# Attention and a gated feed-forward block on one core: the late score rounds, the splits of attention rows and the last two down projections rearranged

## The chip, the cores and the metric

The kernel runs on one core of a Trainium2 chip. The metric is the device time of one execution in microseconds (us). Before the change it is 1312.54 us, the median of three runs (1311.17 to 1313.77). A profile shows one further execution; the engines are called TensorE (PE, with its weight loads as PEld), VectorE (DVE), ScalarE (ACT), GpSimd (POOL) and SyncE (SP, which here only starts DMAs).

## The reference

One input x (2048 rows of 448) goes through two branches, and a gate per row mixes them:

```
g = sigmoid((x * gate_w).sum(-1))
a = attention(x)            # 16 heads of 28, softmax(q k^T / sqrt(28)) v, then @ wo
b = (relu(x W_gate) * (x W_up)) W_down      # 1792 hidden columns
out = g * a + (1 - g) * b
```

All data are float32. The kernel multiplies in a float32 form that keeps fewer bits, so most operands are split into a "high" part (a copy in that form) and a "low" part (the rest), and a product is a sum of a few matmuls of highs and lows.

## The kernel before, in words

Everything is ordered by hand: the program's text gives, engine by engine, the order in which instructions stand, and an engine never passes one of its own that waits. The same holds for the DMA starts on SP and on POOL.

**Projections.** q, k and v are made first and q, k are written to DRAM, from where each head's K and Q are loaded.

**Rounds.** Then come rounds (`ROUNDS`, line 46). A round is a string of letters that TensorE follows:

- `s` is one score matmul (`scores`, line 168): 128 keys by 512 queries into one PSUM bank, then ScalarE's exponential (line 175) into P. Four `s` make a key tile.
- `m` is a pair of matmuls (`smax`, line 139) whose maximum VectorE takes over 128x1024. The maxima of a head are subtracted, by two more rows of K and Q, when its scores are made.
- `x` is one matmul of the feed-forward block (`gu_mm`, line 380). Eleven fill a bank with 128 hidden columns of gate or up for 512 rows; two such units make a hidden tile. After the gate unit comes `relu` (line 391, ScalarE), after the up unit `spill_h` (line 398): a multiply on VectorE and a DMA to DRAM on POOL.

At a round's end the weights of the next units are split (`split_f`, line 364: highs on ScalarE, lows on POOL), and `pv` (line 408) multiplies P and V of the round's key tiles into `po`. A round scores one tile ahead of the tiles whose `pv` ends it; nine slots hold P. `small_things` (line 463) stands every four tiles and starts loads, row sums and the scaling of heads that are done. The last six rounds (`LATE`, line 44) have no maxima left: four tiles and two units each. Their scores alternate between two single banks (`ps_s`) and their units use a half of the double banks (`ps_w`) that the maxima had. `split_wo` (line 454) splits the output projection's weights, highs on ScalarE and lows on POOL, behind the `pv` of tile 248.

**Feed-forward end.** When the rounds are over, their memory is given back and a list (`todo`, line 617) sets the order. It has `gate_up` for the hidden tiles that are left, `down` (line 599: 12 matmuls that add one hidden tile to four banks of 128 rows) for all 56 tiles, in four groups of 512 rows, and for each group `fetch_o` (line 539, SP), two calls of `split_o` (line 546: ScalarE high, POOL low of 128x1024) and four of `wout` (line 553: 11 matmuls with WO, then VectorE's multiplication by the gate). Ahead of `down(i)` stand `fetch_d(i + 4)` (line 581, SP: down weights `wdr`, hidden tile `hr`) and `split_d(i + 2)` (line 589: WD's cast on VectorE and low on POOL, `hh`'s high on ScalarE and low on VectorE). After the last `down` of a group VectorE adds both branches (line 612) and a DMA writes each block of 128 rows.

Of the kernel before, what the change touches and what calls it, by code (L numbers as in the profile page):

```python
# [8 lines left out]
F32 = mybir.dt.float32  # L9
F32R = mybir.dt.float32r  # L10
BF16 = mybir.dt.bfloat16
AF = mybir.ActivationFunctionType
OP = mybir.AluOpType
# [5 lines left out]
P = 128  # L19
S = 2048  # L20
D = 448
# [3 lines left out]
GD = G * DH  # L25
F = 1792
NF = F // P
NB = 4
TB = 512
NK = S // P  # L30
SCALE = DH ** -0.5
# [7 lines left out]
SHORT = "smsxxsmsxsmsxmsxsmsxxsmsxsmsxxsmsxs"  # L39

LONG = "ssmmxsxxsxsmxxsxsmsxxsxxsmmsxxsxxsxsmsxxsmsmsxsxxsxmsmsxxxxsmxssxxmsxsmsxxsmsxmss"
WIDE = "msxxsmsxsxmsxxsxmsxxxxmssmxsxxsxxsmxmssxxxxsxsmsmsxxxxsxsmsxmsxxsxxxsmsmxxxsxsxxxsxmssxmxxss"

LATE = "sxsxxsxsxxsxsxxsxsxxsxsxxsxsxxsxsxsxsx"

ROUNDS = [(SHORT, 0), (SHORT, 1)] + [(LONG, 3)] * 9 + ([(WIDE, 4)] + [(LONG, 3)] * 8) * 2 + [(WIDE, 4)] + [(LATE, 2)] * 6
NP = 9


# [6 lines left out]
PARTS = [(0, 0), (0, 1), (1, 0)]  # L56
# [3 lines left out]
def gated_mix_kernel(ctx, tc, x, wq, wo, wgu, wd, out):  # L60
    nc = tc.nc
# [10 lines left out]
    def ps_s(name):  # L72
        return psum.tile([P, TB], F32, tag="s", bufs=2, name=name)

    def ps_w(name):
        return psum.tile([P, 2, TB], F32, tag="mx", bufs=2, name=name)

    def ps_o(name):
        return psum.tile([P, TB], F32, tag="po", bufs=1, name=name)

    def ps_x(name):
        return psum.tile([P, TB], F32, tag="x", bufs=1, name=name)

    def act_high(dst, src):
        nc.scalar.activation(dst, src, AF.Copy)  # L85
# [4 lines left out]
    def low(dst, src, high):  # L90
        nc.vector.tensor_tensor(dst, src, f32(high), op=OP.subtract)  # L91
# [20 lines left out]
    K = [vp.tile([P, S], F32R, name=f"K{r}") for r in range(3)]  # L112

    def p_slot(k, name, dt=F32):
        if k in (5, 6):
            return V[:, k - 3].rearrange("p k h d -> p (k h d)").rearrange("p (j t) -> p j t", t=TB)
        return (vp if k < 5 else att).tile([P, 4, TB], dt, name=name, tag=f"P{k}", bufs=1)
# [7 lines left out]
    Q = {}  # L125
# [40 lines left out]
    PT = {}  # L166

    def scores(i, j):
        h, kt = divmod(i, NK)
        if j == 0:  # L170
            PT[i] = p_slot(i % NP, f"P_{i}")
        ps = ps_s(f"s_{i}_{j}")
        nc.tensor.matmul(ps, K[h % 3][:GD + 2, kt * P:(kt + 1) * P], Q[h][:GD + 2, j * TB:(j + 1) * TB],  # L173
                         start=True, stop=True)
        nc.scalar.activation(PT[i][:, j], ps, AF.Exp, scale=SCALE)  # L175

    X = {}

# [4 lines left out]
    with tc.tile_pool(name="qkv", bufs=1) as pa:  # L183
# [95 lines left out]
        ps = ps_o("warm_ps")  # L279
# [6 lines left out]
        gate = const.tile([P, 2, NK], F32, name="gate")  # L286
# [74 lines left out]
        WR[i] = fe.tile([P, 2, 4, P], F32, name=f"wgr_{i}", tag="wgr", bufs=2)  # L361
        nc.sync.dma_start(WR[i], wgu[i % NF])

    def split_f(i, low, part=(0, 1)):

        if part[0] == 0:
            WS[i] = fe.tile([P, 2, 7, P], F32R, name=f"wg_{i}", tag="wg", bufs=2)
        w, wr = WS[i], WR[i]
        for s in part:
            act_high(w[:, s, 0:3], wr[:, s, 0:3])  # L370
            low(w[:, s, 3:6], wr[:, s, 0:3], w[:, s, 0:3])
        if part[-1] == 1:
            act_high(w[:, :, 6], wr[:, :, 3])
            low(w[64:, :, 6], wr[64:, :, 3], w[64:, :, 6])
            del WR[i]

# [11 lines left out]

    RL = {}

    def relu(i, ps):
        RL[i] = fe.tile([P, TB], F32, name=f"rl_{i}", tag="rl", bufs=2)
        nc.scalar.activation(RL[i], ps, AF.Relu)

    def hidden(i, ps, h):
        nc.vector.tensor_tensor(h, ps, RL.pop(i), op=OP.mult)  # L396

    def spill_h(i, ps):
        h = fe.tile([P, TB], F32, name=f"h_{i}", tag="h", bufs=2)
        hidden(i, ps, h)  # L400
        h_d[i] = dram.tile([P, TB], F32, name=f"h_d_{i}")
        nc.gpsimd.dma_start(h_d[i], h)  # L402


    NI = H * NK
# [41 lines left out]
    def load_wo():  # L447
        r = f32(q_slot("wor"))
        nc.sync.dma_start(r[:, 0:3, :D], wo_d[0:3 * P].rearrange("(c p) n -> p c n", p=P))
        for a in (0, 64):  # L450
            nc.sync.dma_start(r[a:a + 64, 3, :D], wo_d[3 * P:])
        return r[:, :, :D]
# [6 lines left out]

    done = sum(n for _, n in ROUNDS) // 2  # L460
    nxt = parts = i0 = 0
# [26 lines left out]
    wor = None  # L488
    for r, (order, nu) in enumerate(ROUNDS):
        ni = order.count("s") // NB  # L490
        late = "m" not in order
        todo = list(range(nxt, nxt + nu))
        nxt += nu
        small_things(i0 // 4)
        if m % (2 * NK) == 0 and i0 <= NI - LEAD:
            smax_end(m // (2 * NK) - 1)
        if late and wor is None:
            wor = load_wo()
        ns = nx = 0
        for o in order:  # L500
            if o == "s":
                i, j = i0 + 1 + ns // NB, ns % NB
                if ns == 4 * NB:
                    small_things(i0 // 4 + 1)
                if i < NI:
                    scores(i, j)
                ns += 1
            elif o == "m":
                smax(m)
                m += 1  # L510
            elif nx < NT * nu:
                i, half = divmod(todo[nx // NT], 2)
                if nx % NT == 0:
                    ps = ps_w(f"gu_{i}_{half}")[:, 0] if late else ps_x(f"gu_{i}_{half}")
                gu_mm(ps, i, half, nx % NT)
                nx += 1
                if nx % NT == 0:
                    (spill_h if half else relu)(i, ps)

        ready = nxt + (ROUNDS[r + 1][1] if r + 1 < len(ROUNDS) else 2)  # L520
        ready += ready % 2
        while parts < ready:
            split_f(parts // 2, pool_low, (parts % 2,))
            parts += 1
            if parts % 2 == 0:
                fetch_f(parts // 2 + 1)
        for i in range(i0, i0 + ni):
            pv(i)
            if i == NI - NK // 2:
                split_wo(wor)  # L530
        i0 += ni
# [4 lines left out]
    pf = ctx.enter_context(tc.tile_pool(name="ffn", bufs=1))  # L536
    ON, OR, GA, DR, HH, ACC = {}, {}, {}, {}, {}, {}
# [7 lines left out]

    def split_o(tb, c):
        if c == 0:
            ON[tb] = tuple(pf.tile([P, 4, TB], F32R, name=f"on{k}_{tb}", tag=f"on{k}", bufs=1) for k in range(2))
        c = slice(c, c + 2)
        act_high(ON[tb][0][:, c], OR[tb][:, c])  # L550
        pool_low(ON[tb][1][:, c], OR[tb][:, c], ON[tb][0][:, c])
# [14 lines left out]

    def gate_up(i):
        if i + 1 < NB * NF:
            split_f(i + 1, low)
        if i + 3 < NB * NF:  # L570
            fetch_f(i + 3)
        ps = ps_w(f"gu_{i}")
        for s in range(2):
            for n in range(NT):
                gu_mm(ps[:, s], i, s, n)
        relu(i, ps[:, 0])
        spill_h(i, ps[:, 1])

    WD = pf.tile([P, NF, 2, D], F32R, name="WD")
# [9 lines left out]
    def split_d(i):  # L589
# [6 lines left out]
        act_high(HH[i][:, 0], h)  # L596
        low(HH[i][:, 1], h, HH[i][:, 0])

    def down(i):
        tb, f = divmod(i, NF)  # L600
        if f == 0:
            ACC[tb] = [ps_s(f"acc_{tb}_0"), ps_s(f"acc_{tb}_1"), ps_x(f"acc_{tb}_2"), ps_o(f"acc_{tb}_3")]
        hh = HH.pop(i)
        for t in range(4):
            for n, (a, b) in enumerate(PARTS):
                nc.tensor.matmul(ACC[tb][t][:, :D], hh[:, a, t * P:(t + 1) * P], WD[:, f, b],  # L606
                                 start=(f == 0 and n == 0), stop=(f == NF - 1 and n == 2))
        if f == NF - 1:
            for t in range(4):
                k = tb * 4 + t  # L610
                y = pf.tile([P, D], F32, name=f"y_{k}", tag="y", bufs=4)
                nc.vector.scalar_tensor_tensor(y, ACC[tb][t][:, :D], gate[:, 1, k:k + 1], GA[tb][:, t],
                                               op0=OP.mult, op1=OP.add)
                (nc.sync if tb == NB - 1 else nc.gpsimd).dma_start(out[k * P:(k + 1) * P, :], y)


    todo = [(gate_up, done), (row_sums, H - 1), (gate_up, done + 1)]
# [5 lines left out]
    def before(i, *new):  # L623
        n = todo.index((down, i))
        todo[n:n] = new
# [1 line left out]

    before(0, (spread, H - 1))
    before(1, (normalise, H - 1))
    for tb, load, split, at in ((0, 2, 3, (4, 5, 6, 7)), (1, 5, 8, (10, 11, 14, 14)), (2, 21, 24, (28,) * 4),  # L630
                                (3, 35, 38, (42,) * 4)):
        before(load, (fetch_o, tb))
        before(split, (split_o, tb, 0))
        before(split + 1, (split_o, tb, 2))
        for t, i in enumerate(at):
            before(i, (wout, tb, t))

# [48 lines left out]
```

## Time and profile before

| what | us |
|---|---|
| median of three runs | 1312.54 |
| the profiled execution | 1315.21 |
| its span | 1313.4 |
| six late rounds, first score part to last `po` | 1018.6 to 1097.6 |
| feed-forward end | 1097.6 to 1307.5 |
| last result's work on VectorE ends | 1308.25 |

Busy shares of the span: PE 99%, PEld 69%, DVE 61%, ACT 59%, POOL 27%. A matmul is counted as busy from its start to a modelled end, and the next one overlaps it, so a stretch in which TensorE runs at half its pace can still show as busy: the distance from one start to the next tells more. In the views, a row names the engine, the line of the code, the operation, the tile written and the tiles read; "[0.82 <-ACT on L85]" behind a row means that the engine stood idle for 0.82 us ahead of it, and that ScalarE's write of `on` (line 85 is the helper for all highs on ScalarE, 94 the one for lows on POOL, 88 for casts on VectorE) ended the wait.

### The profile page before, as it was taken

The numbers are of one execution on the slowest core, as the hardware profiler recorded it, in microseconds if no ns is written. First come the engines' busy times: TensorE is split into PE (matmuls) and PEld (weight loads), VectorE is DVE, ScalarE is ACT, GpSimd is POOL, SyncE is SP. The second block draws the span as 40 slices with busy tenths as digits, with TensorE's granted clock in tenths as the row PEclk, the third lists the DMA queues.
The fourth block names the chain that finished last, engine by engine and source line by source line (L and its number), as shares of the span: only waits on it lengthen the run. The fifth ranks groups of instructions, "written<-read, shape, count | busy, mean of one in ns | idle before, by whom it ended". The sixth has DMA issues, their size and how long they took to land.

```text
span 1313.4 us, 17652 instructions
## 1 busy us (share of the span) xinstructions
PE 1300.0 (99%) x6689; PEld 907.0 (69%) x6689; DVE 799.4 (61%) x811; ACT 770.5 (59%) x1454; POOL 360.8 (27%) x496
## 2 busy tenths in 40 slices
PE   9999999999999999999999999999999999999998
PEld 5888666666666666666666666666666556789997
DVE  6577776676767666766767676767666003663332
ACT  5212686667676676766767667676766785222121
POOL 3212113222222232332313222222322235451020
PEclk9999999999999999999999999999999999999999
DMA  8845515142343624142525324151431225534432
GB/s 294 287 166 219 168 58 106 58 110 67 87 86 91 171 63 89 57 97 66 136 68 158 81 72 97 48 105 41 113 108 55 100 64 180 190 114 147 141 103 74
DMA packets 53533, 148.87 MB, mean 113 GB/s; under 512 B 9992, under 2 KB 17096, under 8 KB 48840
## 3 DMA queue, kind: packets, MB, share of 16 engines
q1 hardware_dynamic: 36520, 98.80, 29.2%
q0 software_dynamic: 16928, 48.93, 10.4%
q8 instruction: 53, 0.87, 0.3%
q14 instruction: 32, 0.26, 0.1%
HBM read 102.06 MB, written 46.02 MB: 113 GB/s over the span
## 4 chain that ended last, share of the span: by engine, by line
PE 93%; DMA 3%; issue 1%; DVE 1%; POOL 1%; ACT 1%; SPq 0%; POOLq 0%; ACTq 0%; DVEq 0%
PE gu L383 21%; PE s L173 19%; PE sm L147 18%; PE po L413 17%; PE acc L606 10%; PE qk L253 3%; PE wo L558 3%; PE v L262 2%; DMA K<-qk_d 1%; DMA qk_d<-st 1%; POOL on L94 1%; DMA wr<-wq 0%; DMA xr<-x 0%; DMA wdr<-wd 0%; PE mt L157 0%
## 5 line engine op out<-in xcount | busy, mean ns | idle before, releaser
L149 DVE TENSOR_REDUCE mx<-sm 128x1 f32<-128x1024 f32 x512 | 610.9, 1220 | 189.5 <-PE sm L147 188.3
L175 ACT ACTIVATE P<-s 128x512 f32<-128x512 f32 x800 | 455.0, 597 | 111.1 <-PE s L173 76.1
L173 PE MATMUL s<-Q,K 114*128 114x512 f32 x1024 | 400.7, 405 | 0.4 <-ACT P L175 0.3
L383 PE MATMUL gu<-X,wg 128*128 128x512 f32 x1232 | 397.0, 396 | 0.0
L147 PE MATMUL sm<-K,Q 112*128 112x512 f32 x1024 | 312.2, 396 | 0.7 <-DMA K<-qk_d 0.5
L173 PEld LDWEIGHTS s<-Q,K 114*128 114x128 f32 x1024 | 190.6, 188 | 108.9 <-ACT P L175 53.1
L383 PEld LDWEIGHTS gu<-X,wg 128*128 128x128 f32 x1232 | 233.5, 190 | 43.9 <-issue 0.8
L147 PEld LDWEIGHTS sm<-K,Q 112*128 112x128 f32 x1024 | 193.0, 190 | 46.6 <-DVE mx L149 2.7
L413 PE MATMUL po<-P,V 128*32 128x512 f32 x1600 | 181.9, 594 | 0.0
L94 POOL TENSOR_TENSOR wg<-wgr,wg 128x384 fp32r<-128x384 f32 x153 | 142.2, 941 | 99.8 <-issue 48.7
L175 ACT ACTIVATE V<-s 128x512 f32<-128x512 f32 x224 | 128.2, 598 | 33.2 <-PE s L173 21.2
L402 POOL DMA_DIRECT2D h_d<-h x56 | 31.7, 566 | 412.2 <-DVE h L396 382.0
L606 PE MATMUL acc<-WD,hh 128*128 128x448 f32 x672 | 140.9, 368 | 0.0
L606 PEld LDWEIGHTS acc<-WD,hh 128*128 128x128 f32 x672 | 126.1, 188 | 12.8
L413 PEld LDWEIGHTS po<-P,V 128*32 128x32 f32 x1600 | 49.1, 110 | 110.5 <-issue 110.5
L85 ACT ACTIVATE hh<-hr 128x512 fp32r<-128x512 f32 x56 | 35.2, 631 | 122.4 <-PE acc L606 118.6
L91 DVE TENSOR_TENSOR hh<-hr,hh 128x512 fp32r<-128x512 f32 x56 | 53.7, 960 | 64.4 <-ACT hh L85 64.4
L396 DVE TENSOR_TENSOR h<-gu,rl 128x512 f32<-128x512 f32 x56 | 38.6, 689 | 87.5 <-PE gu L383 37.3
L253 PE MATMUL qk<-X,W 128*128 128x512 f32 x308 | 76.6, 397 | 2.0 <-ACT X L85 1.8
L253 PEld LDWEIGHTS qk<-X,W 128*128 128x128 f32 x308 | 57.3, 188 | 18.4 <-ACT X L85 2.9
L85 ACT ACTIVATE wg<-wgr 128x384 fp32r<-128x384 f32 x168 | 68.0, 489 | 0.0
L413 PE MATMUL po<-V 128*32 128x512 f32 x448 | 54.1, 594 | 0.0
(58 smaller groups left out, 573.6 us busy)
## 6 DMA issues: line engine op xcount, KB each, us to landing
wgr<-wgu SPq DMA_DIRECT2D x56, 512.0 KB
qk_d<-st POOLq DMA_DIRECT2D x28, 512.0 KB, 3.5
K<-qk_d SPq DMA_DIRECT2D x64, 224.0 KB
Q<-qk_d SPq DMA_DIRECT2D x64, 224.0 KB
h_d<-h POOLq DMA_DIRECT2D x56, 256.0 KB, 2.3
hr<-h_d SPq DMA_DIRECT2D x56, 256.0 KB
x_d<-X POOLq DMA_DIRECT2D x6, 1024.0 KB, 5.0
X<-x_d SPq DMA_DIRECT2D x24, 256.0 KB
```

The costliest lines, as they stand in the source:

```text
L85: nc.scalar.activation(dst, src, AF.Copy)
L91: nc.vector.tensor_tensor(dst, src, f32(high), op=OP.subtract)
L94: nc.gpsimd.tensor_tensor(dst, src, f32(high), op=OP.subtract)
L147: nc.tensor.matmul(ps[:, c, :], Q[h][:GD, u * P:(u + 1) * P], K[h % 3][:GD, k0:k0 + TB], start=True, stop=True)
L149: nc.vector.tensor_reduce(MX[h][:, 2 * u + half:2 * u + half + 1], ps, axis=AX.XY, op=OP.max)
L173: nc.tensor.matmul(ps, K[h % 3][:GD + 2, kt * P:(kt + 1) * P], Q[h][:GD + 2, j * TB:(j + 1) * TB], start=True, stop=True)
L175: nc.scalar.activation(PT[i][:, j], ps, AF.Exp, scale=SCALE)
L253: nc.tensor.matmul(ps, W[:, a, c * P:(c + 1) * P], xf(tb, b), start=(n == 0), stop=(n == NT - 1))
L383: nc.tensor.matmul(ps, WS[i][:, s, a], xf(i // NF, b), start=(n == 0), stop=(n == NT - 1))
L413: nc.tensor.matmul(PO[h][32 * j:32 * j + 32], V[:, h // 4 % 2, kt, h % 4], PT[i][:, j], start=(kt == 0), stop=(kt == NK - 1))
L558: nc.tensor.matmul(ps[:, t % 2, :D], ON[tb][b // 4][:, b % 4, t * P:(t + 1) * P], WO[:, a], start=(n == 0), stop=(n == NT - 1))
L606: nc.tensor.matmul(ACC[tb][t][:, :D], hh[:, a, t * P:(t + 1) * P], WD[:, f, b], start=(f == 0 and n == 0), stop=(f == NF - 1 and n == 2))
```

## The change

- Three late rounds of eight tiles and four units take the place of six of four and two. Scores are made in pairs: two matmuls into a double bank, then one exponential of 128x1024. The units use the single banks.
- In the late rounds `relu` and the highs of the weight splits move from ScalarE to VectorE. `split_wo` still stands behind tile 248's `pv`, which is now in the last round.
- The halves of `split_o` move in the list: for rows 0 ahead of the `gate_up` that precedes downs 3 and 4, for rows 1 ahead of downs 7 and 9 (8 and 9 before), rows 2 of 23 and 25 (24 and 25), rows 3 of 37 and 39 (38 and 39). `on` has two buffers for one.
- The last two downs of all, hidden tiles 54 and 55 of the list, run together by blocks of rows: the six matmuls of a block, then its result. The very last block's DMA is started by ScalarE.

```diff
-LATE = "sxsxxsxsxxsxsxxsxsxxsxsxxsxsxxsxsxsxsx"
-ROUNDS = ... + [(LATE, 2)] * 6
+LATE = "ssxxxssxxxssxxxssxx" * 4
+ROUNDS = ... + [(LATE, 4)] * 3
...
+    def scores_pair(i, j):
+        h, kt = divmod(i, NK)
+        if j == 0:
+            PT[i] = p_slot(i % NP, f"P_{i}")
+        ps = ps_w(f"s_{i}_{j}")
+        for c in range(2):
+            nc.tensor.matmul(ps[:, c], K[h % 3][:GD + 2, kt * P:(kt + 1) * P], Q[h][:GD + 2, (j + c) * TB:(j + c + 1) * TB],
+                             start=True, stop=True)
+        nc.scalar.activation(PT[i][:, j:j + 2], ps, AF.Exp, scale=SCALE)
...
-    def split_f(i, low, part=(0, 1)):
+    def split_f(i, high, low, part=(0, 1)):
...
-            act_high(w[:, s, 0:3], wr[:, s, 0:3])
+            high(w[:, s, 0:3], wr[:, s, 0:3])
...
-            act_high(w[:, :, 6], wr[:, :, 3])
+            high(w[:, :, 6], wr[:, :, 3])
...
-        nc.scalar.activation(RL[i], ps, AF.Relu)
+        if late:
+            nc.vector.tensor_scalar_max(RL[i], ps, 0.0)
+        else:
+            nc.scalar.activation(RL[i], ps, AF.Relu)
...
-                    ps = ps_w(f"gu_{i}_{half}")[:, 0] if late else ps_x(f"gu_{i}_{half}")
+                    ps = (ps_s if late else ps_x)(f"gu_{i}_{half}")
...
-            split_f(parts // 2, pool_low, (parts % 2,))
+            split_f(parts // 2, dve_high if late else act_high, pool_low, (parts % 2,))
...
-            ON[tb] = tuple(pf.tile([P, 4, TB], F32R, name=f"on{k}_{tb}", tag=f"on{k}", bufs=1) for k in range(2))
+            ON[tb] = tuple(pf.tile([P, 4, TB], F32R, name=f"on{k}_{tb}", tag=f"on{k}", bufs=2) for k in range(2))
...
+    LAST = range(NB * NF - 2, NB * NF)
...
-        for t in range(4):
-            for n, (a, b) in enumerate(PARTS):
-                nc.tensor.matmul(ACC[tb][t][:, :D], hh[:, a, t * P:(t + 1) * P], WD[:, f, b],
-                                 start=(f == 0 and n == 0), stop=(f == NF - 1 and n == 2))
+        if i not in LAST:
+            for t in range(4):
+                down_mm(i, t)
         if f == NF - 1:
             for t in range(4):
...
+                if i in LAST:
+                    for k in LAST:
+                        down_mm(k, t)
+                result(tb, t, nc.gpsimd if tb < NB - 1 else nc.scalar if t == 3 else nc.sync)
...
-        before(split, (split_o, tb, 0))
-        before(split + 1, (split_o, tb, 2))
+        for k, i in enumerate(split):
+            n = todo.index((down, i))
+            n -= todo[n - 1][0] is gate_up
+            todo.insert(n, (split_o, tb, 2 * k))
```

`down_mm(i, t)` holds the three matmuls of tile i and block t, and `result` the addition and the DMA, as `down` had them.

More of the change, by code (lines that the diff above doesn't have):

```diff
@@ L42 @@
 WIDE = "msxxsmsxsxmsxxsxmsxxxxmssmxsxxsxxsmxmssxxxxsxsmsmsxxxxsxsmsxmsxxsxxxsmsmxxxsxsxxxsxmssxmxxss"
-LATE = "sxsxxsxsxxsxsxxsxsxxsxsxxsxsxxsxsxsxsx"
-ROUNDS = [(SHORT, 0), (SHORT, 1)] + [(LONG, 3)] * 9 + ([(WIDE, 4)] + [(LONG, 3)] * 8) * 2 + [(WIDE, 4)] + [(LATE, 2)] * 6
+LATE = "ssxxxssxxxssxxxssxx" * 4
+ROUNDS = [(SHORT, 0), (SHORT, 1)] + [(LONG, 3)] * 9 + ([(WIDE, 4)] + [(LONG, 3)] * 8) * 2 + [(WIDE, 4)] + [(LATE, 4)] * 3
 NP = 9
@@ L389, in gated_mix_kernel, with relu @@
     RL = {}
-    def relu(i, ps):
+    def relu(i, ps, late=False):
         RL[i] = fe.tile([P, TB], F32, name=f"rl_{i}", tag="rl", bufs=2)
-        nc.scalar.activation(RL[i], ps, AF.Relu)
+        if late:
+            nc.vector.tensor_scalar_max(RL[i], ps, 0.0)
+        else:
+            nc.scalar.activation(RL[i], ps, AF.Relu)
     def hidden(i, ps, h):
@@ L504, in gated_mix_kernel @@
                     small_things(i0 // 4 + 1)
-                if i < NI:
+                if i < NI and not late:
                     scores(i, j)
+                elif i < NI and j % 2 == 0:
+                    scores_pair(i, j)
                 ns += 1
@@ L517, in gated_mix_kernel @@
                 if nx % NT == 0:
-                    (spill_h if half else relu)(i, ps)
+                    spill_h(i, ps) if half else relu(i, ps, late)
         ready = nxt + (ROUNDS[r + 1][1] if r + 1 < len(ROUNDS) else 2)
@@ L568, in gate_up @@
         if i + 1 < NB * NF:
-            split_f(i + 1, low)
+            split_f(i + 1, act_high, low)
         if i + 3 < NB * NF:
@@ L597, in split_d, with down_mm, result @@
         low(HH[i][:, 1], h, HH[i][:, 0])
+    def down_mm(i, t):
+        f = i % NF
+        for n, (a, b) in enumerate(PARTS):
+            nc.tensor.matmul(ACC[i // NF][t][:, :D], HH[i][:, a, t * P:(t + 1) * P], WD[:, f, b],
+                             start=(f == 0 and n == 0), stop=(f == NF - 1 and n == 2))
+    def result(tb, t, queue):
+        k = tb * 4 + t
+        y = pf.tile([P, D], F32, name=f"y_{k}", tag="y", bufs=4)
+        nc.vector.scalar_tensor_tensor(y, ACC[tb][t][:, :D], gate[:, 1, k:k + 1], GA[tb][:, t],
+                                       op0=OP.mult, op1=OP.add)
+        queue.dma_start(out[k * P:(k + 1) * P, :], y)
+    LAST = range(NB * NF - 2, NB * NF)
     def down(i):
@@ L602, in down @@
             ACC[tb] = [ps_s(f"acc_{tb}_0"), ps_s(f"acc_{tb}_1"), ps_x(f"acc_{tb}_2"), ps_o(f"acc_{tb}_3")]
-        hh = HH.pop(i)
-        for t in range(4):
-            for n, (a, b) in enumerate(PARTS):
-                nc.tensor.matmul(ACC[tb][t][:, :D], hh[:, a, t * P:(t + 1) * P], WD[:, f, b],
-                                 start=(f == 0 and n == 0), stop=(f == NF - 1 and n == 2))
+        if i not in LAST:
+            for t in range(4):
+                down_mm(i, t)
         if f == NF - 1:
             for t in range(4):
[L610 to L614, printed above, removed]
+                if i in LAST:
+                    for k in LAST:
+                        down_mm(k, t)
+                result(tb, t, nc.gpsimd if tb < NB - 1 else nc.scalar if t == 3 else nc.sync)
     todo = [(gate_up, done), (row_sums, H - 1), (gate_up, done + 1)]
@@ L629, in gated_mix_kernel @@
     before(1, (normalise, H - 1))
-    for tb, load, split, at in ((0, 2, 3, (4, 5, 6, 7)), (1, 5, 8, (10, 11, 14, 14)), (2, 21, 24, (28,) * 4),
-                                (3, 35, 38, (42,) * 4)):
+    for tb, load, split, at in ((0, 2, (3, 4), (4, 5, 6, 7)), (1, 5, (7, 9), (10, 11, 14, 14)), (2, 21, (23, 25), (28,) * 4),
+                                (3, 35, (37, 39), (42,) * 4)):
         before(load, (fetch_o, tb))
-        before(split, (split_o, tb, 0))
-        before(split + 1, (split_o, tb, 2))
+        for k, i in enumerate(split):
+            n = todo.index((down, i))
+            n -= todo[n - 1][0] is gate_up
+            todo.insert(n, (split_o, tb, 2 * k))
         for t, i in enumerate(at):
```

## The prediction

> **What bounds the kernel now.** I read the busy shares and the chain first, then the table by stretches of time, then the waits of the late stretch, then the order of time where TensorE stands still. Columns of the table: stretch, its length, busy us of PE, PEld, DVE, ACT, POOL, granted clock, DMA share, GB/s.
>
> ```profile
> PE 1300.0 (99%) x6689; PEld 907.0 (69%) x6689; DVE 799.4 (61%) x811; ACT 770.5 (59%) x1454; POOL 360.8 (27%) x496
> ```
> ```profile
> 1028.65:1041.97 13.32, 13.30 (x74) 6.95 (x78) 0.69 (x1) 10.22 (x21) 3.27 (x4) 1.00 0.18 59
> ...
> 1125.00:1170.00 45.00, 41.87 (x195) 36.14 (x194) 29.25 (x27) 10.67 (x17) 22.65 (x16) 1.00 0.45 143
> 1170.00:1300.00 130.00, 130.00 (x632) 118.31 (x632) 48.01 (x68) 30.34 (x46) 19.86 (x18) 1.00 0.39 120
> ```
> ```profile
> PEld s L173 <- ACT P L175: 14.6, 68, 0.4
> ```
> ```profile
> 1138.56 0.97 PE L558 MATMUL wo<-WO,on 128*128 128x448 f32 x4
> 1140.36 1.29 PE L558 MATMUL wo<-WO,on 128*128 128x448 f32 x5 [0.82 <-ACT on L85]
> 1143.38 0.67 PE L558 MATMUL wo<-WO,on 128*128 128x448 f32 x2 [1.74 <-POOL on L94]
> 1143.89 1.40 PE L606 MATMUL acc<-WD,hh 128*128 128x448 f32 x6
> ```
>
> TensorE is the bound everywhere, and "99%" hides the slack because a pipelined matmul counts as busy while the next one waits. So I go by the pitch of starts. Twenty-two gate matmuls without a wait take 5.15 us in the chain (0.234 each), eleven of `wo` 2.25 (0.205 each). Two places are slower than that. First, the six late rounds: a round has 16 scores and 22 gates, 38 x 0.234 = 8.9 us, but its scoring part runs from 1032.15 to 1041.90, 9.75 us, because scores wait for ScalarE (third fence, waits between 1018 and 1098). ScalarE has 16 exponentials at 0.583 (eight back to back take 4.66) and a relu of 0.60 there, 9.9 us. Then 32 `po` matmuls take 3.57. Second, `wo` waits for the split attention rows: the first eleven need 1138.56 to 1143.89, 5.33 instead of 2.25; the next case, at 1165.50, ends 0.84 late. From 1170 to 1300 nothing waits. The granted clock is 1.00.
>
> **Part 1, late rounds: 4.8 us.** Now the six rounds take 1018.56 to 1097.63, 79.07 us. Three rounds of eight tiles hold 76 matmuls (the last has 28 scores, 72). TensorE: 76 x 0.234 = 17.8, plus 0.2 for the two switches between forms (pitches of 0.34 and 0.32 there), plus `po` x64 at 7.00 (the chain has it in every eight-tile round) = 25.0; last round 24.0; the transpose of the maxima 0.3. 25.0 + 25.0 + 24.0 + 0.3 = 74.3, so 4.8 less: about 1.0 from three `po` starts fewer, 3.8 from the stall.
>
> That holds if ScalarE keeps up. The exponential of 128x1024 is not in the trace. It costs at least one of 128x512, 0.60, and at most two back to back, 1.17. The nearest rows are copies on the same engine, 0.631 for 128x512 and 1.047 for 128x1024: 0.42 for the second half, so I take 0.60 + 0.42 = 1.01. Per round 16 x 1.01 = 16.2 against 17.8 on TensorE, and the relus and weight highs leave ScalarE. Per pair: 4.75 matmuls pass between pairs, 1.11 us; pair n+2 reuses the two banks of pair n 2.2 us after its first score, and that pair's scores (0.64) and exponential (1.01) are over after 1.7. Slack 0.5. At 1.17 ScalarE would set the pace: 18.7 a round, about 0.8 over in each of three, 2.4 us.
>
> VectorE gets the relus, two a round: near the 0.68 of a TENSOR_SCALAR 128x448 and the 0.69 of the multiply of 128x512, both from PSUM; I take 0.7. VectorE is idle over 90% of the late rounds, and a gate takes 4.4 us in its bank, with two banks: nothing. Six weight casts a round: the only casts in the trace (128x448) take 0.33 to 1.47. They lie in `po` (7.0 us): nothing, see rival C. Six POOL lows (1.00 for 128x384, 0.74 for 64x256) now stand in one go, 5.5 us, ahead of the DMAs that bring head 15's maxima. Those end near 1023 instead of 1020.8, and the first score of head 15 comes near 1034. Behind the lows also stand the row sums of head 14; their use is half a round later. Nothing.
>
> **A wait that is added.** WO is split behind the last scoring part, no longer one round earlier. Its POOL lows (3.11 and 1.15) follow three weight lows (2.78). The spill of h before them ended 1.8 us after the `po` start in the old last round, so they end about 8.8 after it; `po` ends at 7.0. The first fetch of down weights now waits for them (its buffer lies where `wor` was), and on SP eight fetches of `wdr` and `hr` and two of gate weights stand behind it, 0.2 us later against the end of `po` than now (1.8 against 1099.17 - 1097.63 = 1.54). The first cast of WD is at 6.9 after the end of `po`, and its low ends 0.5 before TensorE wants it. With lows stretched by half the fetch slips 3 to 4 us, of which perhaps 2 would show. Bounds 0 and 2 (a gain is out, since the fetch starts no earlier); I take 0, the row without overlap.
>
> **Part 2, attention rows: 3.9 us.** The first halves go before the gate block that used to precede them (5.15 us of TensorE work), so on ScalarE ahead of a relu that waits for that block. For rows 0: the high (1.05) can start at 1124.6, behind `hh`, its DMA issued at 1117.24; its POOL low (2.4) comes behind one WD low, near 1129. Second half: high behind the relu of 1131.1 and `hh`, 1132.4 to 1133.4, low behind h's spill and WD, to about 1137; TensorE wants it 1.8 us after 1138.34. Slack 3. What is moved past: the next gate weights' highs start 1.05 later and their VectorE lows end near 1130.5 instead of 1128.2; TensorE wants them at 1133.4. The SP fetch of rows 1 waits for the POOL low, so it and the fetches behind it move up too, 1143.4 to about 1137. For rows 1 the double buffer and the earlier place take one low of 2.5 out of the unbroken POOL run 1159.92 to 1169.58. Gains 3.08 + 0.84 = 3.9. Next late: nothing the trace shows; from 1143.9 on the casts, lows and `hh` of the next downs keep TensorE's own pace, and they are not issued later. Halves of rows 2 and 3 move inside the stretch that never waits: nothing.
>
> **Part 3, the end: 0.3 us.** The last two downs take the same 24 matmuls (4.9 us), by blocks. The last result still needs the last matmul (ends 1307.53), 0.63 on VectorE and a DMA. The first three results start up to 1.9 us earlier, but they were not what kept the last one waiting: SP's four issues (2.19 in all) fit between results 0.63 apart. What is left is the DMA's tail: bulk packets end near 1309.8, and a trickle of 5 to 23 GB/s goes on to 1312.0. The DMA view has one 16 KB instruction packet among the results, and one engine's share of two results seems to stand behind it. With results earlier only one would. Bounds: -0.6 (the last issue is ScalarE's first, and SP's first packet at the kernel's start came 1.46 after issue against 0.84 here) and 2.2 (the packet falls elsewhere); I take 0.3, half a result's eight packets of 0.074. The Trainium skill ("DMA: Bandwidth & Descriptors", "Issuing engines are not separate DMA queues") says that another issuing engine saves only the time of issue; here SP's issue is not backed up, so by it this step alone is worth 0.
>
> **Sum.** 4.8 + 3.9 + 0.3 = 9.0. The profiled execution took 1315.21 (span 1313.4 and 1.8 around it), 2.7 above the median of 1312.54; I take the difference from both: 1306.2 there, 1303.5 as a median.
>
> **Rivals.**
> - A, the `wo` wait only changes hands: POOL or a fetch ends as late as before. For it: POOL's unbroken run. Against: 3 us of slack. Part 2 gives nothing: 1307.4.
> - B, the wide exponential saves nothing (1.17): 2.4 lost, 1305.9. Against: the two copies.
> - A and B together: 1309.8.
> - C, slower: VectorE's casts and POOL's lows block each other in the weight splits of the first two late rounds. For it: casts of 0.38 take 1.35, and lows of 1.16 take 1.53, where they overlap after 1159. Each of these rounds has six pairs in a row from 0.9 us after `po` begins, and TensorE wants the last at 7.0 + 8.9 + 3.6 = 19.5 (`po`, half a scoring part, ten gates of the next block). So it costs from 3.1 us a pair on, and the kernel is slower than before from 3.9 on (9.0 lost over twelve pairs); the longest rows end to end make 1.47 + 1.45 = 2.9. At 4.1 it loses 12: 1315.5. This is also what the Trainium skill warns of ("GPSIMD Engine Reference", "Key points"): POOL shares its SBUF interfaces with VectorE and contends with its two-port modes. The overlapped rows agree with that; the sum stays.
> - D, the instruction packet misses the results: 2.0 more, 1301.5.
>
> **How the numbers follow.** Forecast 0.68 (1302.3 to 1305), A 0.11, B 0.07, both 0.03, C 0.05, D 0.06. The range 1301.3 to 1307.6 holds the forecast, A, B and D. A measurement can tell about 0.2%, 2.6 us: only C is slower, only A with B is within it. Faster 0.92, same 0.03, slower 0.05.
>
> **What would show it.** Right: late rounds near 25.0 us, exponentials near 1.0, scores without waits on ScalarE, `wo` blocks of 2.25 throughout. Wrong: exponentials of 1.17 (B); `wo` still waiting (A); gate loads that wait for POOL or VectorE (C); a late first `wdr` with the first down waiting; a clock under 1.00.

## The result and the profile after

The changed kernel takes 1303.16 us, the median of six runs (1302.74 to 1303.69), against 1312.05 of the kernel before beside it. The ratio is 0.9932, with a 95% interval of 0.9919 to 0.9945: 8.9 us less (7.2 to 10.6). The forecast was 1303.5.

The table by stretches of the changed kernel, from one start of `po` to the next and then around the split attention rows (columns as in the prediction):

```profile
1010.71:1035.68 24.97, 24.97 (x145) 16.26 (x149) 4.08 (x8) 19.17 (x26) 9.50 (x14) 1.00 0.33 111
1035.68:1060.66 24.98, 24.98 (x145) 16.25 (x148) 5.22 (x11) 16.90 (x18) 10.05 (x14) 1.00 0.21 75
1060.66:1084.77 24.11, 24.11 (x140) 15.40 (x144) 6.53 (x11) 15.63 (x16) 9.13 (x12) 1.00 0.23 76
...
1117.00:1162.00 45.00, 45.00 (x214) 39.90 (x213) 22.16 (x28) 12.80 (x20) 23.96 (x16) 1.00 0.48 163
```

An eight-tile round takes 24.97 us, where two of four tiles took 2 x 13.32. In the 45 us around the attention rows PE is busy throughout; before, it lacked 3.13. The waits of the late rounds, and the groups by shape there (count, then busy us, mean ns):

```profile
PEld s L184 <- ACT P L186: 0.3, 1, 0.3
```
```profile
L186 ACT ACTIVATE P<-s 128x1024 f32<-128x1024 f32 x38 | 38.5, 1026 | 3.7 <-PE s L184 1.3
...
L94 POOL TENSOR_TENSOR wg<-wgr,wg 128x384 fp32r<-128x384 f32 x10 | 10.2, 1038 | 0.4
...
L405 DVE TENSOR_SCALAR rl<-gu 128x512 f32<-128x512 f32 x6 | 4.1, 692 | 30.5 <-PE gu L394 30.5
...
L88 DVE CAST wg<-wgr 128x384 fp32r<-128x384 f32 x10 | 4.0, 439 | 0.0
```

Scores waited 14.6 us for ScalarE before, 68 times; now 0.3, once. The wide exponential is 1.026 us. The chain, start and length, shows the output projection without a wait:

```profile
1127.64 5.15 PE gu L394 x22
1132.79 2.25 PE wo L574 x11
1135.04 2.47 PE acc L618 x12
1137.51 2.25 PE wo L574 x11
```

The two profiled executions differ by more than the medians, 1315.21 to 1303.16. I split both, and every kernel below, at three points: the transpose of the last maxima, the first gate matmul behind the last `po`, and the end of the last matmul.

| kernel | to the late rounds | late rounds | from there to the last matmul's end | to the span's end |
|---|---|---|---|---|
| before | 1018.56 | 79.07 | 209.89 | 5.9 |
| changed | 1017.64 | 74.06 | 205.96 | 3.7 |
| before, once more | 1018.55 | 79.07 | 211.17 | 3.7 |
| late rounds alone | 1019.14 | 74.08 | 209.85 | 3.7 |
| attention rows alone | 1018.87 | 79.08 | 205.95 | 3.7 |
| end alone | 1017.93 | 79.08 | 211.23 | 3.7 |

The first column is the same code in all of them and moves by some 3 us between executions (1016.4 to 1019.9 over all fourteen profiles), so a step is read inside its own stretch: 5.0 us in the late rounds, 3.9 behind them. The last column's 2.2 us came from an instruction packet, as the next section shows. In the DMA view of before, over its last six microseconds, it is the one packet that is not a result's; of the changed kernel the order of time shows the last result and the start of its DMA:

```profile
q8 instruction: 1, 0.02, 2.1%
```
```profile
1297.69 0.68 DVE L624 SCALAR_TENSOR_TENSOR y<-acc,gate,ga 128x448 f32<-128x448 f32 x1 [0.56 <-PE acc L618]
1298.41 0.38 ACTq L626 DMA_DIRECT2D out<-y  x1
```

### The profile page after: what moved, and what is told of

It is laid out like the page before. It is cut to its first block, busy times and chain, and to the rows that moved or that the text cites. A ratio compares the mean times of both kernels' runs of the same rounds, so it can differ in the third digit from the quotient of the medians.

```text
span 1301.4 us, 17614 instructions
## 1 busy us (share of the span) xinstructions
PE 1293.2 (99%) x6689; PEld 913.2 (70%) x6689; DVE 799.9 (61%) x832; ACT 758.6 (58%) x1387; POOL 359.9 (28%) x496
## 3 DMA queue, kind: packets, MB, share of 16 engines
q0 software_dynamic: 16928, 48.93, 10.2%
## 4 chain that ended last, share of the span: by engine, by line
PE 96%; DMA 2%; DVE 1%; ACT 1%; issue 0%; SPq 0%; ACTq 0%
PE gu L394 22%; PE sm L147 18%; PE po L427 17%; PE s L173 17%; PE acc L618 11%; PE qk L264 4%; PE wo L574 3%; PE v L273 2%; PE s L184 2%; DMA ls<-os 1%; DMA xr<-x 1%; DVE mx L149 1%; DMA qk_d<-st 1%; PE mt L157 0%; ACT st L85 0%; DVE st L91 0%
## 5 line engine op out<-in xcount | busy, mean ns | idle before, releaser
L175 ACT ACTIVATE P<-s 128x512 f32<-128x512 f32 x724 | 413.0, 597 | 103.2 <-PE s L173 71.2
L394 PE MATMUL gu<-X,wg 128*128 128x512 f32 x1232 | 389.6, 396 | 0.0
L173 PE MATMUL s<-Q,K 114*128 114x512 f32 x932 | 361.2, 403 | 0.2 <-ACT P L175 0.2
L173 PEld LDWEIGHTS s<-Q,K 114*128 114x128 f32 x932 | 173.2, 188 | 87.1 <-ACT P L175 38.7
L175 ACT ACTIVATE V<-s 128x512 f32<-128x512 f32 x208 | 119.3, 597 | 30.0 <-PE s L173 18.6
L91 DVE TENSOR_TENSOR hh<-hr,hh 128x512 fp32r<-128x512 f32 x56 | 43.5, 777 | 64.5 <-ACT hh L85 64.5
L85 ACT ACTIVATE wg<-wgr 128x384 fp32r<-128x384 f32 x153 | 61.7, 490 | 0.0
L91 DVE TENSOR_TENSOR mh<-mr,mh 16x128 fp32r<-16x128 f32 x16 | 4.5, 279 | 82.6 <-ACT mh L161 82.6
```

The lines of the kernel that those rows point to most:

```text
L394: nc.tensor.matmul(ps, WS[i][:, s, a], xf(i // NF, b), start=(n == 0), stop=(n == NT - 1))
```

## The experiments

Twelve kernels ran. Five executions or more of each were timed beside the kernel before; ratios are to that kernel, since that kernel's own median lay between 1312.05 and 1314.65 from one set of runs to another. My theory was that the parts are independent and add up, that the two stalls are all of the gain, and that the end is worth nothing. The rivals were that a part works only with another, that a different resource decides, or that the end's shorter tail is real.

**One part at a time.** Only the late rounds, with the old `down` and the old places of the splits put back into the changed kernel:

```diff
-    for tb, load, split, at in ((0, 2, (3, 4), (4, 5, 6, 7)), (1, 5, (7, 9), (10, 11, 14, 14)), ...
+    for tb, load, split, at in ((0, 2, 3, (4, 5, 6, 7)), (1, 5, 8, (10, 11, 14, 14)), ...
...
-    ... tag=f"on{k}", bufs=2)
+    ... tag=f"on{k}", bufs=1)
```

> Only the late rounds (three of eight tiles, paired scores, relus and weight highs on VectorE); attention rows and the end as before. Theory: the parts add up, so this one gives the 5.0 us that its stretch is shorter by in the two traces (79.07 to 74.06): 1307.0 us. Rival: what is gained here is partly lost at the output projection's wait for the split rows, which then comes earlier against the fetches: 1308 to 1309, with more than 3.9 us of waits there.

Measured: ratio 0.9968 (0.9955 to 0.9981), late rounds 74.08, the rest 209.85 as before. The loss that the rival expects on top does not show: the waits of `wo` stand there unchanged:

```profile
PEld wo L574 <- POOL on L94: 3.1, 2, 2.1
PE wo L574 <- POOL on L94: 2.3, 2, 1.7
```

Only the attention rows:

```diff
-    for tb, load, split, at in ((0, 2, 3, (4, 5, 6, 7)), (1, 5, 8, (10, 11, 14, 14)), ...
+    for tb, load, split, at in ((0, 2, (3, 4), (4, 5, 6, 7)), (1, 5, (7, 9), (10, 11, 14, 14)), ...
...
-    ... tag=f"on{k}", bufs=1)
+    ... tag=f"on{k}", bufs=2)
```

> Only the attention rows' splits moved and their second buffer; late rounds and the end as before. Theory: 4.0 us less (209.90 to 205.90 from the last po to the last matmul), 1308.0 us. Rival: the move pays only together with the earlier fetches that the new late rounds bring, less than 3 us.

Measured: 0.9967 (0.9954 to 0.9980), late rounds 79.08, the rest 205.95, to 0.01 us the changed kernel's. So both parts stand alone, and together they make the whole: 4.2 and 4.3 us by the ratios, 5.0 and 3.9 by the stretches, 8.9 in the changed kernel.

Only the end:

```diff
-        for t in range(4):
-            for n, (a, b) in enumerate(PARTS):
-                nc.tensor.matmul(ACC[tb][t][:, :D], hh[:, a, ...
+        if i not in LAST:
+            for t in range(4):
+                down_mm(i, t)
...
+                result(tb, t, nc.gpsimd if tb < NB - 1 else nc.scalar if t == 3 else nc.sync)
```

> Only the last two downs by blocks of rows, and the last DMA started by ScalarE. Theory: nothing to be gained, since the last result waits for the last matmul either way; 1311.7 to 1312.1 us, and the 2.1 us by which the end is shorter in the changed kernel's profile come from an instruction packet that did not fall among its results. Rival: the 2.1 us are real in every run, 1310.0 us.

Measured: 0.9997 (0.9989 to 1.0006), no difference. The end took 3.7 us from the last matmul, as in every old and new kernel whose results no instruction packet met. But the stretch before it was 1.3 us longer than in the first profile of before, with the same waits in it. That called for the old kernel once more:

> The kernel before once more, unchanged. Theory: 79.1 us of late rounds and, behind them, 209.9 us to the last matmul or 1.3 us more, as the clock falls to half for 3.4 us after the wait for the split rows in some executions (it did with only the end changed) and not in others; 3.7 us from the last matmul to the end, or more where the instruction packet falls among the results. Rival: both are fixed with a program, then 209.9 and 5.9 as in the first profile.

Measured: 1.0003 (0.9994 to 1.0012). The stretch was 211.17 and the tail 3.7. So neither belongs to a program. The stretches of this execution around the waits for the split rows show the cause:

```profile
1138.00:1142.90 4.90, 2.81 (x13) 1.83 (x11) 3.05 (x3) 2.06 (x3) 2.51 (x2) 1.00 0.14 54
1142.90:1146.30 3.40, 2.93 (x8) 2.63 (x9) 2.06 (x1) 0.00 (x0) 1.51 (x2) 0.50 0.49 157
1146.30:1150.00 3.70, 3.70 (x20) 3.41 (x19) 0.00 (x0) 0.63 (x1) 0.00 (x0) 1.00 0.96 318
```

Right behind the waits the granted clock (eighth column) is 0.50 for 3.4 us, with 8 matmuls where full speed would do some 15. In two of the four profiles that have these waits the clock fell, in two it did not. The mean clock of the timed executions points the same way: it was below 1.000 in 45 of 70 executions with these waits (the kernel before, the late rounds alone, the end alone), and in 6 of 41 of the eight kernels that have neither these waits nor those for lows done more than once. A mean does not tell where in an execution the clock fell.

**The last DMA on SyncE again:**

```diff
-                result(tb, t, nc.gpsimd if tb < NB - 1 else nc.scalar if t == 3 else nc.sync)
+                result(tb, t, nc.gpsimd if tb < NB - 1 else nc.sync)
```

> The changed kernel with the very last result's DMA started by SyncE again, on the queue of the three before it. Theory: the same within 0.1 us, since SyncE is free when the last result is ready: from the last matmul's end to the span's end 3.7 us. Rival: ScalarE's empty queue is quicker, 0.3 us or more.

Measured: 3.63 us from the last matmul to the end; 0.9924 (0.9909 to 0.9938). The queue makes no difference. What did make one is the packet: over fourteen profiles the tail was 3.6 to 3.7 us except in two, in which an instruction packet started 1.0 and 1.2 us after the last matmul, among the results: 5.9 (before) and 4.7 (relus on ScalarE, below). In the others it came earlier, later or not at all. The packets themselves show the delay. In the profile of before the instruction packet ends at 1310.54; sixteen result packets of 1792 bytes, two results' share of one DMA engine, start one behind the other from 1310.53 to 1311.95, when all others have ended by 1309.85. With the relus on ScalarE eight such packets, one result's share, stand behind it.

**One buffer for the split rows** in the changed kernel, the places in the list as they are there:

```diff
-    ... tag=f"on{k}", bufs=2)
+    ... tag=f"on{k}", bufs=1)
```

> The changed kernel with one buffer for the split rows instead of two; the places in the list stay. Theory: the moves carry most of it, and the buffer only the second wait (0.84 us): 1303.9 to 1304.1 us, with the wait back at rows 1 alone, since their first split waits again for the output projection of rows 0. Rival: the place alone is enough, 1303.2 us.

Measured: 0.9932 (0.9920 to 0.9944), the same as with two. In the 45 us around the rows PE is busy throughout, and one weight load waits there for 0.2 us:

```profile
1117.00:1162.00 45.00, 45.00 (x214) 39.65 (x213) 23.58 (x28) 12.19 (x19) 23.74 (x16) 1.00 0.49 166
```
```profile
PEld wo L574 <- POOL on L94: 0.2, 1, 0.2
```

My theory was wrong and the rival right: the place in the list is enough. The second buffer lets the first low of rows 1 run at 1144.8 instead of 1150.3 on GpSimd, and hardly anything hangs on it: one block of `wo` takes 2.34 us instead of 2.25, and the stretch to the last matmul 206.07 instead of 205.96.

**What lifts ScalarE's bound.** Eight-tile rounds with relus and highs on VectorE, but single banks:

```diff
-LATE = "ssxxxssxxxssxxxssxx" * 4
+LATE = "sxsxxsxsxxsxsxxsxsxxsxsxxsxsxxsxsxsxsx" * 2
...
-                if i < NI and not late:
+                if i < NI:
                     scores(i, j)
...
-                    ps = (ps_s if late else ps_x)(f"gu_{i}_{half}")
+                    ps = ps_w(f"gu_{i}_{half}")[:, 0] if late else ps_x(f"gu_{i}_{half}")
```

> The changed kernel, but the scores of the late rounds as before in single banks with an exponential of 128x512 each (and the units in a half of the double banks); eight tiles a round, relus and weight highs on VectorE. Theory: ScalarE's throughput decides. 32 x 0.583 = 18.7 us and a start of 0.6 against 18.0 on TensorE: some 0.9 us in each of the two full rounds, nothing in the last (28 scores, 16.3 us), so 1304.9 us. Rival: the turnover of the two banks decides, and the whole stall of before stays, 1.4 us a round of eight tiles, 3.8 in all: 1307.0 us.

Measured: late rounds 77.11, 3.0 more than with pairs and 2.0 less than before; ratio 0.9948 (0.9936 to 0.9961). The wait of before is back:

```profile
PEld s L173 <- ACT P L175: 14.9, 74, 0.4
```

The scoring parts are 19.2, 19.1 and 17.8 against 17.9, 18.0 and 17.1, so 1.3, 1.1 and 0.7 more. Throughput explains them, though not by my sum: 18.7 and a start of 0.6 make 19.3, which is 1.3 over TensorE's 18.0 and not 0.9. And the last round, where I had said nothing, has its 28 scores in the first seven eighths of the string: 16.3 us of exponentials and the six gates behind them (1.4) make 17.7, so ScalarE sets the pace there too. The rival's 3.8 is not reached.

The other half, pairs with relus and highs on ScalarE:

```diff
-                    spill_h(i, ps) if half else relu(i, ps, late)
+                    spill_h(i, ps) if half else relu(i, ps)
...
-            split_f(parts // 2, dve_high if late else act_high, pool_low, (parts % 2,))
+            split_f(parts // 2, act_high, pool_low, (parts % 2,))
```

> The changed kernel with the relus and the weight highs of the late rounds on ScalarE again; the pairs stay. Theory: the pairs alone lift the bound; ScalarE has 16 x 1.03 + 2 x 0.6 = 17.6 us in a scoring part of 18.0, and the highs lie in po: 1303.2 us, at most 0.4 more. Rival: each relu pushes the next exponential out by 0.6, over the slack of 0.5, and TensorE cannot get it back: some 0.3 to 0.6 at each of six relus, 1305 to 1306.7 us.

Measured: 74.01 us of late rounds; 0.9930 (0.9918 to 0.9943). One round, ScalarE's busy time in the sixth column:

```profile
1041.84:1066.83 24.99, 24.99 (x145) 16.18 (x141) 2.14 (x4) 19.78 (x25) 9.77 (x15) 1.00 0.26 75
```

So with the relus and highs on ScalarE the pairs (and fewer `po` starts) make all of the gain, and the rival's 0.3 to 0.6 at each relu does not show; beside the pairs, what was moved to VectorE costs nothing and brings nothing.

**How much slack the weight splits have.** Twice and four times the lows in the first two late rounds, in the changed kernel. The last chunk's low works in place, so an even number of passes puts the high back there. That holds for four passes as well, although the second expectation here speaks of the same values, and for the WO lows done twice below: all three kernels leave that low out of their weights, and run the same instructions otherwise.

```diff
+    def pool_low_again(dst, src, high):
+        for _ in range(4):      # 2 in the other kernel
+            pool_low(dst, src, high)
...
-            split_f(parts // 2, dve_high if late else act_high, pool_low, (parts % 2,))
+            split_f(parts // 2, dve_high if late else act_high,
+                    pool_low_again if late and r + 1 < len(ROUNDS) else pool_low, (parts % 2,))
```

> The changed kernel with every weight low at the end of the first two late rounds done twice. The last chunk's low works in place, so its second pass puts the high back: that part of the hidden layer's weights is computed differently. Theory: the lows end at 1.7 + 11.8 = 13.5 us after po begins, TensorE wants the last at 19.5: nothing, late rounds 74.1 us, 1303.2. Rival: the first hidden tile's own three lows, wanted at about 11, or the casts on VectorE, stretched by GpSimd, cost something already, late rounds over 75 us.

> The changed kernel with every weight low at the end of the first two late rounds done four times over on GpSimd (the same values written again). Theory of the prediction: six lows take 5.9 us, begin 1.7 us after po does, and TensorE wants the last at 19.5. Four times over they end at 1.7 + 23.6 = 25.3, 5.8 us late in each of two rounds: 1314.8 us. Rival: what stands behind the lows on GpSimd (spills, row sums) or the casts on VectorE is what hurts, from fewer lows on, and more is lost: over 1318 us.

Measured: twice 74.08, nothing (0.9922, 0.9908 to 0.9935); four times 87.89, 13.8 more (1.0034, 1.0022 to 1.0047). The waits of the late rounds with four times, and a stretch behind one of them:

```profile
PEld gu L398 <- POOL wg L94: 10.0, 3, 4.1
```
```profile
1060.70:1064.10 3.40, 3.40 (x8) 2.67 (x9) 0.00 (x0) 1.02 (x1) 1.07 (x2) 0.50 0.70 188
```

The lows of a round take 23.57 us and TensorE waits for them alone. By starts it loses 5.3 in the first round (5.8 expected, though 2.4 of it already when the first hidden tile's third low is wanted) and 3.9 in the second; the other 4.6 go with spells of half clock behind the waits (3.4 and 6.8 us long). So the splits have room for twice the lows and not for four times, as the prediction had worked out. The waits come to 9.2 where 11.6 were expected, and the clock, which was not in the sum, makes the price of overstepping larger all the same.

**The added wait.** WO's lows done twice in one kernel, and WO split one round earlier in another:

```diff
+        for _ in range(2):
+            pool_low(WO[:, 3:6], r[:, 0:3], WO[:, 0:3])
...
+        for _ in range(2):
+            pool_low(WO[64:, 6], r[64:, 3], WO[64:, 6])
```

```diff
-            if i == NI - NK // 2:
+            if i == NI - NK:
                 split_wo(wor)
```

> The changed kernel with both lows of the output projection's weights done twice (4.3 us more on GpSimd), so that the first fetch of down weights starts some 6.1 us after the end of po instead of 1.8. Theory: there was slack in this wait; of 4.3 us, 0.5 to 2 show, as the first down waits for hh or WD: 1303.7 to 1305.2 us. Rival 1: no slack, all of it shows: 1307.5 us. Rival 2: all of it is hidden, 1303.2 us.

> The changed kernel with the output projection's weights split in the middle late round instead of the last, so that the first fetch of down weights waits for po alone. Theory: nothing, since the first down of the changed kernel does not wait; 1303.2 us, and the fetch starts 0.2 to 0.7 us earlier against the end of po. Rival: GpSimd, with six weight lows and these two in one round, makes TensorE wait there: more than 0.5 us.

The start of the first fetch of down weights in the changed kernel and with the early split, where the last `po` gives way to gates at 1091.70 and 1092.76:

```profile
1093.57 0.33 SPq L601 DMA_DIRECT2D wdr<-wd  x1
```
```profile
1092.92 0.33 SPq L601 DMA_DIRECT2D wdr<-wd  x1
```

Split early, the fetch starts 0.2 us behind `po` instead of 1.9, more than the 0.7 that I had allowed, and nothing follows from it: 205.97 us to the last matmul against 205.96 (0.9925, 0.9912 to 0.9937). Done twice, the fetch starts at 6.7 and that stretch is 3.8 longer (0.9936, 0.9922 to 0.9949, in which this loss does not stand out from the spread of the runs). TensorE's order of time shows the waits, and the next stretch the clock:

```profile
1103.33 0.48 PE L620 MATMUL acc<-WD,hh 128*128 128x448 f32 x1 [1.05 <-ACT hh L85]
1104.13 4.10 PE L620 MATMUL acc<-WD,hh 128*128 128x448 f32 x11 [0.33 <-POOL WD L94]
```
```profile
1105.00:1108.00 3.00, 3.00 (x10) 2.69 (x9) 2.94 (x7) 1.05 (x2) 0.95 (x2) 0.56 1.06 353
```

By starts, 2.2 us are waits for `hh` and WD, just over the theory's 0.5 to 2, and the other 1.6 the slower clock. So of 4.8 us that the fetch slipped some 2.6 were covered as far as waits go, but with the clock 3.8 were lost, which is nearer to rival 1 than to the theory.

## Why the prediction was right, step by step

- **Late rounds, 4.8 forecast, 5.0 measured.** Mechanism and size hold. A round was to take 25.0 and takes 24.97 and 24.98; the exponential was to take 1.01 and takes 1.026. One reason given was too much: that relus and highs leave ScalarE is not needed, the pairs are enough. Rival B's premise (the pair saves nothing) is out by that row, and its price was too low: with two narrow exponentials the loss is 3.0, not 2.4, with 1.3 and 1.1 in the full rounds, where 0.8 was taken.
- **The added wait, 0 forecast, 0 measured.** The fetch starts 1.9 us after `po` ends (1.8 forecast). The 2 us that I gave for a slip of 3 to 4 is about what a slip of 4.8 costs in waits; the clock, 1.6 more in that profile, was not in it.
- **Attention rows, 3.9 forecast, 3.9 measured.** The second low of rows 0 was to end near 1137, 39.4 us after the last `po` (1097.6 before); it ends at 1130.9, 39.2 after (1091.7 here). The part played by the second buffer was wrong; it is worth 0.1. And in executions in which the clock falls behind the wait the gain is 5.2, which I did not foresee.
- **The end, 0.3 forecast, nothing measured.** The step that failed is the packet: I took it to be there in each execution and to meet one result instead of two. It met the results in two of fourteen profiles, and in one of two of the same kernel before. Where it met the new end, one result's packets stood behind it, as the term supposed. Here the Trainium skill's rule on issuing engines ("DMA: Bandwidth & Descriptors", "Issuing engines are not separate DMA queues"), by which the other queue is worth nothing as long as SyncE's issues do not hold the results up, agrees with the runs: 3.63 on SyncE, 3.7 on ScalarE.
- **From the profile to the median.** The profiled execution of before had the packet's 2.2 us in it, and the one of after did not. So the sum taken from the median holds, 1303.5 against 1303.16, and the sum taken from the profiled time does not, 1306.2 against 1303.16. The 8.7 of the two parts that hold come from stretches in which the packet does not lie.
- **How near it came.** That the sum of 9.0 meets the measured 8.9 so closely is in part luck: the interval is 7.2 to 10.6, and the five variants whose stretches are the changed kernel's within 0.2 us took 8.9 to 10.2 us less than the kernel before beside them. The half clock behind the waits, in the kernel before alone, would raise the gain in this way; the sum has no term for it.
- **Rivals.** A is out (no waits of `wo`), C is out (the six lows of the changed kernel end 7.6 us after `po` begins, where TensorE wants the last at 19.5, and twice the lows cost nothing), and D, the packet that misses, is true of the profile but not of the median.

## What to carry to other kernels

Where the busiest engine shows 99%, count the starts of its instructions in each stage against their pitch elsewhere; two stalls hidden that way made the whole forecast here, and each could be tested alone. A wait for an instruction that stands late in another engine's order can be ended, as here, by an earlier place in that order, with hardly any help from a further buffer. And make the sum inside a stage, because two executions of one kernel differ in other places by as much as a small change is worth.

## What the hardware showed that was not expected

TensorE's clock fell to half for 3.41 us after short waits: pauses of 1.18 and 2.10 us from one start to the next, in two of four executions (the end alone and the kernel before once more), or of 1.44, 0.80 and 0.55 in a row, with WO's lows done twice. It cost 1.3 to 1.6 us. With four times the lows a pause of 3.09 us was followed by 3.41 us of half clock and one of 4.11 by 6.83, and one of 2.65 by none. What decides between them stays open. The Trainium skill ("TensorE: Matmul & The Clock Gate", "Part 1: The HAM clock gate") gives a window of about 3.4 us that runs on its own and a return to half clock after an idle one; the length of the spells agrees with it, the condition does not: in the end alone, the kernel before once more and WO's lows done twice TensorE was never idle for that long at once ahead of the spell, the longest being about 1.7 us.

One instruction packet of 16 KB among the last results lengthened the end by 1.1 and 2.2 us, in one profile each: one DMA engine's result packets stood behind it.
